# Value and sum products of four heads on four 32-column PE tiles, double attention steps, and a first batch turned by the PE

## The chip, the cores and the metric

The kernel runs on one core of a Trainium2 chip. The metric is device time in microseconds (us) of one execution, as a median of several runs; a profile of one execution goes with every kernel. PE is TensorE (matmul), PEld its weight loads, DVE is VectorE, ACT is ScalarE, POOL is GpSimd, SP is SyncE, which here only issues DMA.

## The reference

Causal attention with 16 extra "beacon" keys that every query sees, then a feed-forward network (FFN) with a gate. Everything comes in float32; the kernel computes in bfloat16 with float32 sums.

```python
B, H, S, Nb, D = 8, 8, 576, 16, 64            # batches, heads, tokens, beacons, head size
scores = (q @ concat(beacon_k, k).T) / sqrt(D) # causal mask on the last S keys
a = exp(scores - max) ; a /= a.sum()
x = (a @ concat(beacon_v, v))                  # -> 4608 tokens x 512 channels
out = (relu(x @ w_gate) * (x @ w_val)) @ w_out # 512 -> 1536 -> 512
```

## The kernel before

Scores are made with keys on the partitions, so that the exponentials `e` can be the moving operand of the value product without a transposition. An attention step handles one pair of heads and one or two key tiles: score matmuls (two row halves of PE, one for each head), one exponential on ACT, masks on POOL; one step later the value and sum products. A batch has 16 steps. One group of FFN work (eight matmuls "up", or twelve "down") is put into each step.

```python
def qk(pr, i):                                   # scores: 64 rows of PE for each head
    s = s_ps.tile([P, 2, 512], FP32, name="s")
    for (kt, q0, n, c, _, _) in STEPS[i]:
        for a in range(2):
            rows = slice(a * D, (a + 1) * D)
            nc.tensor.matmul(s[:, a, c:c + n], pr.batch.kT[rows, pr.p, kt * P:(kt + 1) * P],
                             pr.batch.qT[rows, pr.p, q0:q0 + n], start=True, stop=True)
...
def av(pr, i):                                   # values and sums: two tiles of 64 columns
    ...
        for part in range(2):
            for a in range(2):
                rows = slice(a * D, (a + 1) * D)
                w = pr.batch.v[:kr, kt, c0:c0 + D] if part == 0 else ones[:kr, :]
                nc.tensor.matmul(o[rows, part, q0 - cq0:q0 - cq0 + n], w, e[:kr, a, c:c + n], ...)
    if i == last:
        nc.vector.reciprocal(r[:, :cn], o[:, 1, :cn])
        nc.vector.tensor_mul(xT[:, pr.p, t0:t0 + cn], o[:, 0, :cn], r[:, :cn])
        nc.sync.dma_start(rsum[g:g + 2, cq0:cq0 + cn], ...)      # for a range check at the end
                                                                 # (the general path behind it is not taken here)
...
def up(self, nf, c0, c1):                        # FFN: two accumulators from a ring of two banks
    g = f_ps.tile([P, M_TILE], FP32, name="f")   # four matmuls with wg
    nc.scalar.activation(gs[:, :n], g[:, :n], AF.Relu)
    u = f_ps.tile([P, M_TILE], FP32, name="f")   # four matmuls with wv
    nc.vector.tensor_mul(self.h[:, nf, c0:c1], gs[:, :n], u[:, :n])
...
# K and Q, all batches: load (SP) -> cast to bf16 -> DMA transpose (SP)
nc.sync.dma_start_transpose(dst[:, :, t * P:t * P + n], self.h[x, t][:n])
# step s: scores and exponential of step s, one FFN group, value products of step s - 1
```

Of the kernel before, what the change touches and what calls it, by code (L numbers as in the profile page):

```python
# [15 lines left out]








STEPS = (
    ((0, 0, 240, 0, 112, 16), (1, 112, 128, 240, 128, 0)),
    ((0, 240, 256, 0, 0, 0), (1, 240, 256, 256, 0, 0)),
    ((2, 240, 256, 0, 128, 0), (3, 368, 128, 256, 128, 0)),
    ((0, 496, 80, 0, 0, 0), (1, 496, 80, 80, 0, 0), (2, 496, 80, 160, 0, 0),
     (3, 496, 80, 240, 0, 0), (4, 496, 80, 320, 80, 0)),
)  # L30
STEP_COLS = (368, 512, 384, 400)

CHUNKS = ((0, 240, 0, 0), (240, 256, 1, 2), (496, 80, 3, 3))
CHUNK_OF_STEP = (0, 1, 1, 2)


def general_path(tc, q, k, v, beacon_k, beacon_v, out, ident, wg, wv, wo):
# [76 lines left out]
    x_b = xT_dram.rearrange("(b ko e) d s -> b (e d) ko s", b=B, e=2)  # L114
    out_b = out.rearrange("(b s) n -> b s n", b=B)
    HALF = S // 2
    with tc.tile_pool(name="gen_sb2", bufs=1) as sb, \
# [3 lines left out]
        for ki in range(KM):  # L121
            nc.sync.dma_start(x[:, ki], x_b[bass.ds(i, 1), :, ki].rearrange("o p s -> (o p) s"))
# [12 lines left out]
        for t in range(NT):  # L135
            n = min(P, S - t * P)
            op = ps.tile([P, d_model], FP32, name="g_op")
            for nf in range(NF):
                nc.tensor.matmul(op[:n], hT[:, nf, t * P:t * P + n], wo[:, nf, :],
                                 start=(nf == 0), stop=(nf == NF - 1))  # L140
            ob = sb.tile([P, d_model], FP32, name="g_ob")
            nc.vector.tensor_copy(ob[:n], op[:n])
            nc.sync.dma_start(
                out_b[bass.ds(i, 1), t * P:t * P + n].rearrange("o s n -> (o s) n"), ob[:n])

@with_exitstack
def kernel(
# [23 lines left out]
    TAIL = Stot - 4 * P  # L171
    M_TILE = 512
    scale = 1.0 / (D ** 0.5)
    assert (Nb, S, D) == (16, 576, 64)
# [4 lines left out]
    ones = const.tile([P, D], BF16, name="ones")  # L179
# [5 lines left out]

    rsum = const.tile([2 * B * NP, S], FP32, name="rsum")
# [5 lines left out]
    psb = main.enter_context(tc.tile_pool(name="psb", bufs=3))  # L192
    nrm = main.enter_context(tc.tile_pool(name="nrm", bufs=3))
# [3 lines left out]
    o_ps = main.enter_context(tc.tile_pool(name="o_ps", bufs=2, space=bass.MemoryType.PSUM))  # L197
    f_ps = main.enter_context(tc.tile_pool(name="f_ps", bufs=2, space=bass.MemoryType.PSUM))



    class Batch:
# [28 lines left out]
        def cast(self, x, t, copy):  # L231
            n = self.rows(x, t)
            if x == "v":
                dst = self.v[:n, t]
            else:
                h = self.h[x, t] = half.tile([P, d_model], BF16, name="half")
                dst = h[:n]
            copy(dst, self.raw[x, t][:n])  # L238

        def turn(self, x, t):  # L240
            n = self.rows(x, t)
            dst = self.qT if x == "q" else self.kT
            nc.sync.dma_start_transpose(dst[:, :, t * P:t * P + n], self.h[x, t][:n])  # L243
# [3 lines left out]
    def load_w(dst, src, n0, n1):  # L247
        nc.gpsimd.dma_start(dst[:, :, n0:n1],
                            src.rearrange("(ko ki) n -> ki ko n", ki=P)[:, :, n0:n1])


    class Pair:
        def __init__(self, batch, p):
            self.batch, self.p = batch, p
            self.s, self.e, self.o = {}, {}, {}

    def qk(pr, i):
        s = s_ps.tile([P, 2, 512], FP32, name="s")
        for (kt, q0, n, c, _, _) in STEPS[i]:
            for a in range(2):  # L260
                rows = slice(a * D, (a + 1) * D)
                nc.tensor.matmul(s[:, a, c:c + n],  # L262
                                 pr.batch.kT[rows, pr.p, kt * P:(kt + 1) * P],
                                 pr.batch.qT[rows, pr.p, q0:q0 + n], start=True, stop=True)
        pr.s[i] = s

    def softmax(pr, i):
        n = STEP_COLS[i]
        e = psb.tile([P, 2, 512], BF16, name="e")
        nc.scalar.activation(e[:, :, :n], pr.s[i][:, :, :n], AF.Exp, scale=scale)  # L270
        for (kt, q0, _, c, m, base) in STEPS[i]:
            if m:
                nc.gpsimd.affine_select(  # L273
                    out=e[:, :, c:c + m], in_=e[:, :, c:c + m],
                    pattern=[[0, 2], [1, m]], compare_op=ALU.is_ge, fill=0.0,
                    base=base, channel_multiplier=-1)
        pr.e[i] = e

    def av(pr, i):
        ci = CHUNK_OF_STEP[i]  # L280
        cq0, cn, first, last = CHUNKS[ci]
        if i == first:
            pr.o[ci] = o_ps.tile([P, 2, 256], FP32, name="o")
        o = pr.o[ci]
        e = pr.e[i]
        for j, (kt, q0, n, c, _, _) in enumerate(STEPS[i]):
            kr = min(P, Stot - kt * P)
            for part in range(2):
                for a in range(2):
                    rows = slice(a * D, (a + 1) * D)  # L290
                    c0 = (2 * pr.p + a) * D
                    w = pr.batch.v[:kr, kt, c0:c0 + D] if part == 0 else ones[:kr, :]
                    nc.tensor.matmul(  # L293
                        o[rows, part, q0 - cq0:q0 - cq0 + n], w, e[:kr, a, c:c + n],
                        start=(i == first and j == 0 and part == 0),
                        stop=(i == last and j == len(STEPS[i]) - 1),
                        skip_group_check=True)
        if i == last:
            r = nrm.tile([P, 256], FP32, name="r")
            nc.vector.reciprocal(r[:, :cn], o[:, 1, :cn])  # L300
            t0 = pr.batch.b * S + cq0
            nc.vector.tensor_mul(xT[:, pr.p, t0:t0 + cn], o[:, 0, :cn], r[:, :cn])  # L302
            g = 2 * (pr.batch.b * NP + pr.p)
            nc.sync.dma_start(rsum[g:g + 2, cq0:cq0 + cn],  # L304
                              r.rearrange("(a x) n -> a x n", a=2)[:, 0, :cn])


    class Ffn:
# [21 lines left out]
        def down(self, ms):  # L330
# [7 lines left out]
            nc.sync.dma_start(out[m:m + P, :], ob)  # L338

        def groups(self, c0, c1, d0, d1):  # L340
            return ([lambda nf=nf: self.up(nf, c0, c1) for nf in range(NF)]
                    + [lambda ms=ms: self.down(ms) for ms in range(d0, d1)])

    def count_in_range():

        rows = 2 * B * NP
# [6 lines left out]
        cnt_ps = o_ps.tile([1, 1], FP32, name="o")  # L353
# [6 lines left out]

    ffn_tiles = [Ffn(m * M_TILE) for m in range(n_tokens // M_TILE)]
    W_PARTS = 4
    weights = [lambda d=d, s=s, c=c: load_w(d, s, c * (d_ff // W_PARTS), (c + 1) * (d_ff // W_PARTS))
               for c in range(W_PARTS) for d, s in ((wg, moe_w_gate), (wv, moe_w_val))]
    weights.append(lambda: load_w(wo, moe_w_out, 0, d_model))

    with tc.manual_schedule():
        batches = [Batch(0)]
        copies = {"k": nc.vector.tensor_copy, "q": nc.scalar.copy, "v": nc.gpsimd.tensor_copy}
        for u in UNITS[:6]:  # L370
            batches[0].load(*u)
        for u in UNITS[:6]:
            batches[0].cast(*u, copies[u[0]])
            if u[0] != "v":
                batches[0].turn(*u)
        for w in weights[:2]:
            w()
        for u in UNITS[6:]:
            batches[0].load(*u)


# [5 lines left out]
        for j, u in enumerate(UNITS[6:]):  # L387
            at(j // 3, lambda u=u: batches[0].cast(*u, copies[u[0]]))
            if u[0] != "v":
                at(j // 3, lambda u=u: batches[0].turn(*u))  # L390
        for j, w in enumerate(weights[2:]):
            at(j, w)

        def fetch(b, s0):
            at(s0, lambda: batches.append(Batch(b)))
            for j, u in enumerate(UNITS):
                s = s0 + j * 3 // 4
                at(s, lambda u=u: batches[b].load(*u))
                at(s + 2, lambda u=u: batches[b].cast(*u, nc.gpsimd.tensor_copy))
                if u[0] != "v":  # L400
                    at(s + 3, lambda u=u: batches[b].turn(*u))

        work, ready = [], {}
        for b in range(B):
            for c, (_, _, first, last) in enumerate(CHUNKS):
                for p in range(NP):
                    for i in range(first, last + 1):
                        work.append((b, p, i))
                done = (b * S + CHUNKS[c][0] + CHUNKS[c][1])
                ready[len(work)] = done  # L410
            if b + 1 < B:
                fetch(b + 1, 16 * b + (1 if b else 3))


        spans = [(0, 240), (240, 512)] + [(m, m + M_TILE) for m in range(M_TILE, n_tokens, M_TILE)]
        queue, have, pairs = [], 0, {}
        LAG = 1
        for s in range(len(work) + LAG):
            if s - LAG in ready:
                have = ready[s - LAG]  # L420
# [5 lines left out]
            for act in later.pop(s, []):  # L426
                act()
            if s < len(work):
                b, p, i = work[s]
                pr = pairs.setdefault((b, p), Pair(batches[b], p))  # L430
                qk(pr, i)
                softmax(pr, i)
            if queue:
                queue.pop(0)()
# [42 lines left out]
```

## Time and profile before

| kernel before | |
|---|---|
| time | 477.17 us, median of 3 (474.74 to 478.57) |
| profiled span | 476.9 us |
| PE busy | 407.7 us, 85% |
| DVE, ACT, POOL busy | 235.9, 197.5, 132.9 us |

Three parts of the profile page of the kernel before: busy time by engine, and the span in 40 slices of 11.9 us (a digit is the busy share in tenths; PEclk is the clock granted to PE).

```profile
PE 407.7 (85%) x3454; PEld 198.3 (42%) x3505; DVE 235.9 (49%) x322; ACT 197.5 (41%) x290; POOL 132.9 (28%) x293
...
PE   0043748979999999999999999999999999799994
...
PEclk9999759979999999999999999999999999899998
...
GB/s 164 188 200 195 162 184 117 133 194 102 111 119 194 96 104 151 160 83 112 155 161 91 112 139 167 79 123 175 127 95 3 1 24 68 0 1 88 1 18 76
```

There are two regimes. For about 80 us PE is idle for long stretches, and DMA moves 160 to 200 GB/s for most of that time. From there to the end PE is full. So a change must either shorten the start or take PE time away.

The waits of PE in the first 100 us of the kernel before (who waited for what: us in all, times, longest) show what the start waits for, and the windows show each 20 us of it (columns: busy us of PE, PEld, DVE, ACT, POOL with counts, granted clock, DMA share, GB/s).

```profile
PE o L293 <- POOL e L273: 26.8, 8, 8.4
PE s L262 <- DMA qT<-half: 18.3, 2, 17.2
```

```profile
20.00:40.00 20.00, 6.09 (x53) 3.63 (x53) 9.62 (x11) 6.40 (x9) 9.71 (x18) 1.00 1.34 198
40.00:60.00 20.00, 13.07 (x105) 7.72 (x104) 6.66 (x10) 6.48 (x11) 4.82 (x9) 0.83 1.24 180
60.00:80.00 20.00, 11.64 (x170) 8.08 (x171) 7.91 (x13) 5.58 (x10) 8.37 (x17) 0.74 1.05 167
```

The first score product waits 17.2 us for a turned Q; after that the value products wait for masks.

One step in the steady stretch, from the timeline of PE of the kernel before (start, us until the modelled end, line, matmul, how many):

```profile
229.94 0.30 PE L293 MATMUL o<-e,v 128*64 128x256 bf16 x2
230.07 0.28 PE L293 MATMUL o<-e,ones 128*64 128x256 bf16 x2
230.18 0.28 PE L293 MATMUL o<-e,v 128*64 128x256 bf16 x2
230.29 0.28 PE L293 MATMUL o<-e,ones 128*64 128x256 bf16 x2
230.50 0.39 PE L262 MATMUL s<-qT,kT 64*128 64x256 bf16 x4
230.83 1.04 PE L320 MATMUL f<-xT,wg 128*128 128x512 bf16 x4
231.70 1.03 PE L326 MATMUL f<-xT,wv 128*128 128x512 bf16 x4
232.66 0.30 PE L293 MATMUL o<-e,v 128*64 128x256 bf16 x2
```

Read it by the starts, since the ends overlap. A pair of 256-column value matmuls takes 0.11 us and then the next pair starts; four 512-column FFN matmuls take 0.87 us. From the start of the last quartet (231.70) to the next value matmul (232.66) it is 0.96 us instead of 0.87: about 0.1 us is lost where the shape of the tiles changes, and again from values to scores and from scores to FFN.

The two groups of the kernel before that the change aims at, beside the FFN (line, engine, operation, count, busy us, mean ns of one, idle time before and its releaser):

```profile
L300 DVE RECIPROCAL r<-o 128x240 f32<-128x240 f32 (+2 forms) x96 | 130.0, 1354 | 89.0 <-PE o L293 86.5
...
L293 PE MATMUL o<-e,v 128*64 128x80 bf16 (+3 forms) x704 | 66.6, 246 | 33.4 <-POOL e L273 33.4
```

### The profile page before, as it was taken

The page shows a single profiled execution, that of the slowest core. Times are in us where ns is not written, and L with a number is a line of the kernel's source. Part 1 is how long each engine was busy: PE and PEld are TensorE (multiplying, and loading weights), DVE is VectorE, ACT ScalarE, POOL GpSimd, SP SyncE. Part 2 cuts the span into 40 slices and gives each one's busy share as a digit, 9 for nine tenths or more (in the row PEclk, how much of TensorE's full clock was granted, in tenths as well). Part 3 has the DMA queues.
Part 4 walks back from the last instruction along what each step waited for, and adds up shares of the span by engine and source line. Part 5 has one row for each costly group of instructions (what it writes and reads, how often), then busy time and mean ns, then how long its engine had stood idle before and what let it go on. Part 6 is the DMA issues. An engine that isn't in the chain of part 4 may idle for free.

```text
span 476.9 us, 9059 instructions
## 1 busy us (share of the span) xinstructions
PE 407.7 (85%) x3454; PEld 198.3 (42%) x3505; DVE 235.9 (49%) x322; ACT 197.5 (41%) x290; POOL 132.9 (28%) x293
## 2 busy tenths in 40 slices
PE   0043748979999999999999999999999999799994
PEld 0022425545444444444444444444444444244442
DVE  0052426745486357546663766286528653330320
ACT  2132414534455455445544555455545543132321
POOL 2171235444234333423351334143411110000000
PEclk9999759979999999999999999999999999899998
DMA  9999998695359337934892498258720001002002
GB/s 164 188 200 195 162 184 117 133 194 102 111 119 194 96 104 151 160 83 112 155 161 91 112 139 167 79 123 175 127 95 3 1 24 68 0 1 88 1 18 76
DMA packets 166145, 53.37 MB, mean 112 GB/s; under 512 B 155728, under 2 KB 161488, under 8 KB 166096
## 3 DMA queue, kind: packets, MB, share of 16 engines
q1 hardware_dynamic: 160320, 48.01, 50.2%
q0 software_dynamic: 5776, 4.72, 7.0%
q8 instruction: 29, 0.48, 0.4%
q14 instruction: 20, 0.16, 0.1%
HBM read 38.27 MB, written 9.44 MB: 100 GB/s over the span
## 4 chain that ended last, share of the span: by engine, by line
PE 57%; DMA 20%; SPq 9%; DVE 5%; POOL 4%; issue 3%; ACT 0%; POOLq 0%; DVEq 0%; ACTq 0%
PE f L333 20%; PE f L320 13%; PE f L326 12%; DMA raw<-in_k_dram 12%; PE o L293 8%; DMA raw<-in_q_dram 6%; SPq L220 5%; PE s L262 4%; DVE r L300 3%; SPq L243 3%; DMA raw<-in_v_dram 2%; POOL half L238 2%; POOL e L273 2%; SPq L304 1%; DVE xT L302 1%
## 5 line engine op out<-in xcount | busy, mean ns | idle before, releaser
L300 DVE RECIPROCAL r<-o 128x240 f32<-128x240 f32 (+2 forms) x96 | 130.0, 1354 | 89.0 <-PE o L293 86.5
L270 ACT ACTIVATE e<-s 128x736 bf16<-128x736 f32 (+3 forms) x128 | 110.5, 864 | 135.9 <-PE s L262 125.7
L328 DVE TENSOR_TENSOR hT<-g,f 128x512 bf16<-128x512 f32 (+2 forms) x120 | 75.6, 630 | 110.0 <-PE f L326 98.1
L320 PE MATMUL f<-xT,wg 128*128 128x512 bf16 (+2 forms) x453 | 116.3, 369 | 5.3 <-DVE xT L302 3.1
L326 PE MATMUL f<-xT,wv 128*128 128x512 bf16 (+2 forms) x473 | 115.4, 365 | 1.6 <-ACT g L323 0.7
L333 PE MATMUL f<-wo,hT 128*128 128x512 bf16 x415 | 96.5, 380 | 1.5 <-issue 1.0
L293 PE MATMUL o<-e,v 128*64 128x80 bf16 (+3 forms) x704 | 66.6, 246 | 33.4 <-POOL e L273 33.4
L273 POOL TENSOR_SCALAR_AFFINE_SELECT e<-e 128x256 bf16<-128x256 bf16 (+2 forms) x160 | 58.9, 387 | 106.4 <-ACT e L270 106.2
L323 ACT ACTIVATE g<-f 128x512 f32<-128x512 f32 (+2 forms) x120 | 66.3, 553 | 43.4 <-PE f L320 39.5
L293 PEld LDWEIGHTS <-v 128*64 128x64 bf16 (+1 forms) x704 | 38.0, 112 | 84.0 <-issue 82.6
L326 PEld LDWEIGHTS <-wv 128*128 128x128 bf16 x480 | 48.1, 100 | 57.0 <-issue 12.1
L238 POOL CAST half<-raw 128x512 bf16<-128x512 f32 (+1 forms) x70 | 42.7, 611 | 88.2 <-DMA raw<-in_q_dram 39.3
L262 PE MATMUL s<-qT,kT 64*128 64x80 bf16 (+2 forms) x704 | 47.4, 239 | 18.3 <-DMA qT<-half 18.3
L293 PE MATMUL o<-e,ones 128*64 128x80 bf16 (+3 forms) x704 | 61.3, 238 | 0.0
L320 PEld LDWEIGHTS <-wg 128*128 128x128 bf16 x480 | 40.1, 100 | 47.3 <-issue 17.8
L333 PEld LDWEIGHTS <-hT 128*128 128x128 bf16 x432 | 40.0, 98 | 46.8 <-issue 0.8
L336 ACT COPY ob<-f 128x512 f32<-128x512 f32 x36 | 21.1, 586 | 70.0 <-PE f L333 67.0
L238 POOL CAST v<-raw 128x512 bf16<-128x512 f32 (+1 forms) x40 | 24.5, 611 | 66.9 <-DMA raw<-in_v_dram 66.8
L293 PEld LDWEIGHTS <-ones 128*64 128x64 bf16 (+1 forms) x704 | 36.5, 114 | 0.2
L302 DVE TENSOR_TENSOR xT<-o,r 128x240 bf16<-128x240 f32 (+2 forms) x96 | 34.3, 358 | 3.3
L262 PEld LDWEIGHTS <-kT 64*128 64x128 bf16 x704 | 18.5, 97 | 33.5 <-issue 25.2
L238 DVE CAST half<-raw 128x512 bf16<-128x512 f32 (+1 forms) x5 | 2.3, 460 | 21.6 <-DMA raw<-in_k_dram 21.6
(19 smaller groups left out, 17.0 us busy)
## 6 DMA issues: line engine op xcount, KB each, us to landing
out_dram<-ob SPq DMA_DIRECT2D x36, 256.0 KB
raw<-in_q_dram SPq DMA_DIRECT2D x32, 256.0 KB
raw<-in_k_dram SPq DMA_DIRECT2D x24, 256.0 KB
raw<-in_v_dram SPq DMA_DIRECT2D x24, 256.0 KB
raw<-in_k_dram SPq DMA_DIRECT2D x8, 224.0 KB
raw<-in_v_dram SPq DMA_DIRECT2D x8, 224.0 KB
wg<-in_moe_w_gate_dram POOLq DMA_DIRECT2D x4, 384.0 KB, 6.1
wv<-in_moe_w_val_dram POOLq DMA_DIRECT2D x4, 384.0 KB, 7.6
```

The lines of the kernel that those rows point to most:

```text
L238: copy(dst, self.raw[x, t][:n])
L262: nc.tensor.matmul(s[:, a, c:c + n], pr.batch.kT[rows, pr.p, kt * P:(kt + 1) * P], pr.batch.qT[rows, pr.p, q0:q0 + n], start=True, stop=True)
L270: nc.scalar.activation(e[:, :, :n], pr.s[i][:, :, :n], AF.Exp, scale=scale)
L273: nc.gpsimd.affine_select(out=e[:, :, c:c + m], in_=e[:, :, c:c + m], pattern=[[0, 2], [1, m]], compare_op=ALU.is_ge, fill=0.0, base=base, ...
L293: nc.tensor.matmul(o[rows, part, q0 - cq0:q0 - cq0 + n], w, e[:kr, a, c:c + n], start=(i == first and j == 0 and part == 0), stop=(i == la ...
L300: nc.vector.reciprocal(r[:, :cn], o[:, 1, :cn])
L302: nc.vector.tensor_mul(xT[:, pr.p, t0:t0 + cn], o[:, 0, :cn], r[:, :cn])
L320: nc.tensor.matmul(g[:, :n], wg[:, ki, nf * P:(nf + 1) * P], x[:, ki], start=(ki == 0), stop=(ki == KM - 1))
L323: nc.scalar.activation(gs[:, :n], g[:, :n], AF.Relu)
L326: nc.tensor.matmul(u[:, :n], wv[:, ki, nf * P:(nf + 1) * P], x[:, ki], start=(ki == 0), stop=(ki == KM - 1))
L328: nc.vector.tensor_mul(self.h[:, nf, c0:c1], gs[:, :n], u[:, :n])
L333: nc.tensor.matmul(o, self.h[:, nf, ms * P:(ms + 1) * P], wo[:, nf, :], start=(nf == 0), stop=(nf == NF - 1))
```

## The change

The intent has four parts. (1) Values and sums of four heads run on four tiles of 32 columns: three parts (lower half of the values, upper half, sums) instead of two parts for each of two pairs, so three column times where there were four. (2) Steps are twice as large: 7 a batch instead of 16, with about 4.5 us of FFN work in each; value products are made for a whole chunk (240, 256 or 80 queries of four heads) at once, when all its key tiles are done. (3) K and Q of the first batch are loaded in halves and turned by PE (matmul with an identity) instead of DMA transposes. (4) One reciprocal serves four heads: 48 instead of 96, of the same length. A consequence: the channels lie in another order on the partitions, so the gate and value weights come in four loads of 32 partitions each where one load was enough. Smaller changes of the order of work came with it (more buffers for the exponentials, other steps for loads and casts, later stores).

```diff
-        for part in range(2):
-            for a in range(2):
-                rows = slice(a * D, (a + 1) * D)
-                w = pr.batch.v[:kr, kt, c0:c0 + D] if part == 0 else ones[:kr, :]
-                nc.tensor.matmul(o[rows, part, ...], w, e[:kr, a, c:c + n], ...)
+                for part in range(3):
+                    for hh in range(4):
+                        rows = slice(hh * C, (hh + 1) * C)            # C = 32
+                        c0 = (2 * hh + self.g) * D + part * C
+                        w = ones[:kr, :] if part == 2 else self.batch.v[:kr, kt, c0:c0 + C]
+                        o = self.os[rows] if part == 2 else self.ab[rows, part]
+                        nc.tensor.matmul(o[:, ...], w, e[:kr, 2 * (hh % 2) + hh // 2], ...)
 ...
     def load_w(dst, src, n0, n1):
-        nc.gpsimd.dma_start(dst[:, :, n0:n1], src.rearrange("(ko ki) n -> ki ko n", ki=P)[:, :, n0:n1])
+        for hh in (0, 2, 1, 3):
+            nc.gpsimd.dma_start(dst[hh * C:(hh + 1) * C, :, n0:n1],
+                src[hh * P:(hh + 1) * P, n0:n1].rearrange("(k p) n -> p k n", p=C))
 ...
+        def turn_half(self, x, i, cast, move):           # first batch only
+            ... cast to bf16 ...
+            for r in range(2):
+                for j in range(NP):
+                    nc.tensor.transpose(ps[:, j, r], h[:, r, j * P:(j + 1) * P], ident)
+            move(dst[...], ps.rearrange("a j r p -> a j p r"))
 ...
+    STEPS = 7
+    QUOTA = 4.5
+        # step: scores of two units, first exponential; values of the finished chunks, reciprocal;
+        #       FFN groups for about 4.5 us, after the first of them scaling and second exponential
+                if u[0] != "v":
+                    at(s + (1 if b == 1 else 2), lambda u=u: batches[b].turn(*u))
```

## The prediction

> **What bounds it now.** PE is busy 407.7 of 476.9 us (busy table). By windows, the first 100 us hold only about 50 us of PE work, part of it at a granted clock of 0.74 to 0.83; from 100 to 400 us PE is busy 94 to 99%. In the chain of waits the start is DMA (raw K, Q loads, DMA transposes); the first score matmul starts at 17.2 us, waiting for the transposed Q; value products wait 33.4 us for the mask on POOL, 14 times, up to 8.4 us. After that PE is the limit.
>
> In the steady stretch (timeline, 204 to 250 us) a step takes about 2.6 us: eight FFN matmuls at 0.217 us (1.74), values and sums 0.32 to 0.43, scores 0.16 to 0.21, and 0.33 left at the three changes of tile shape (about 0.1 us between the last FFN matmul's end and the first value matmul, and so on). The Trainium skill ("TensorEngine Tiling (Array Packing)", Key Properties) says a change of tiling mode drains the engine; these gaps agree. With 128 steps that is about 42 us. DVE reciprocals take 130 us; PE hardly waits for them.
>
> **What changes, costed.**
> 1. 56 steps for 128: 72 x 0.33 = 24 us of shape changes saved. Several FFN groups now stand back to back; in the FFN-only end a group takes 1.87 us, not 1.74, because the second accumulator waits for the DVE product: 5 to 7 us given back.
> 2. Values and sums: now 1664 columns x 2 parts on two tiles, about 1.43 us a pair, 46 us in all. On four tiles 1664 x 3 parts for 16 groups would stream in 33 us. But loads and matmuls rise from 2816 to 4224; an 80-column pair takes 36 ns for four instructions, so eight in 33 ns may not fit. I estimate 38 to 44 us: gain about 5, all on PE. The skill ("TensorE: Matmul & The Clock Gate", Part 3) measured 2.38 times for three column tiles, also below ideal.
> 3. Reciprocals: 48 instead of 96 of the same length, DVE -65 us, off the critical path, worth almost nothing.
> 4. Start: K and Q of batch 0 by PE; first score matmul at 11 to 12 us. But FFN cannot start before step 3, and needs weights: 34 issues instead of 9, in POOL's queue; from the second group on, each waits for an earlier one's landing (6 to 8 us measured), with masks and casts behind it. So POOL will stall value products until 50 to 60 us. DMA, about 180 GB/s, is full there in both kernels. I expect 8 to 18 us gained over the first 100 us.
> 5. Later waits for POOL shrink by some microseconds.
>
> **Sum.** 477 - 24 + 6 - 5 - 13 - 6 = 435; I say 434 us, range 412 to 454 (8 in 10). Chances: faster 0.94, within 2% 0.04, slower 0.02.
>
> **What would show it.** (1) In the steady stretch a step of about 6 us, a batch of 42 us instead of 46, the same 0.3 us of gaps per step. (2) Four 256-column value matmuls in about 0.11 us, four 80-column ones in 0.05 to 0.07. (3) DVE busy near 165 us. (4) First score matmul near 11 us; waits for POOL masks and weights before 60 us.
>
> **What would make it wrong.** Four-column tiles that don't overlap (values over 60 us: then only 3 to 5% faster); POOL blocked by weights for longer, so batch 1 starts late; a throttled clock in the denser stretch. Conversely, if POOL keeps up and weights land early, 410 us.

## The result, and the profile after

The changed kernel took 442.77 us (median of 4, 441.67 to 442.96) against 477.87 us (median of 4, 474.74 to 478.62) for the kernel before on the same chip. The ratio is 0.926, with an interval from 0.923 to 0.930.

The same parts of the page, now of the changed kernel; a slice is 11.0 us:

```profile
PE 384.0 (87%) x4202; PEld 198.1 (45%) x4253; DVE 174.9 (40%) x232; ACT 190.7 (43%) x272; POOL 132.5 (30%) x242
...
PE   3487552898799999999999999999999999699994
...
PEclk9999765699699999999999999999999999999999
...
GB/s 240 222 115 189 132 152 165 164 180 149 82 156 168 100 137 189 141 101 175 166 105 117 156 167 128 120 147 187 120 64 3 2 73 26 0 25 71 1 26 77
```

PE now starts at once, but a hole opens in the fifth to seventh slice (44 to 77 us), where the granted clock also falls. DMA moved 240 GB/s in the first slice and only 115 in the third.

Waits of PE in the first 100 us of the changed kernel, the four longest, and the windows that answer to those of before:

```profile
PE f L412 <- DMA wo<-in_moe_w_out_dram: 8.1, 2, 5.8
PE f L291 <- DVE half L288: 7.6, 3, 3.6
PE s L322 <- DMA qT<-half: 5.7, 1, 5.7
PE ab L364 <- POOL e L338: 3.7, 1, 3.7
```

```profile
20.00:40.00 20.00, 15.37 (x165) 10.74 (x166) 10.23 (x16) 8.68 (x14) 18.83 (x35) 1.00 1.05 142
40.00:60.00 20.00, 10.13 (x109) 6.23 (x110) 4.71 (x8) 3.05 (x6) 4.61 (x7) 0.75 0.99 166
60.00:80.00 20.00, 8.32 (x194) 5.38 (x193) 1.96 (x4) 5.10 (x6) 7.94 (x15) 0.59 0.62 131
```

The mask waits are nearly gone. In their place PE waits for weights, for one turned tile of the second batch, and for rows of the first (of the 7.6 us, 3.1 are the first wait of all, for the beacon keys, and 4.5 are for the last rows). From 20 to 40 us POOL is busy 18.8 of 20 us.

One step of the changed kernel in its steady stretch, PE's timeline (each `ab` line holds the two value parts of four heads, each `os` line their sums):

```profile
218.79 0.52 PE L322 MATMUL s<-qT,kT 64*128 64x80 bf16 x12
219.25 0.40 PE L364 MATMUL ab<-e,v 128*32 128x256 bf16 x8
219.47 0.28 PE L364 MATMUL os<-e,ones 128*32 128x256 bf16 x4
219.58 0.39 PE L364 MATMUL ab<-e,v 128*32 128x256 bf16 x8
...
222.25 1.03 PE L399 MATMUL f<-xT,wg 128*128 128x512 bf16 x4
223.26 1.02 PE L405 MATMUL f<-xT,wv 128*128 128x512 bf16 x4
224.22 0.61 PE L322 MATMUL s<-qT,kT 64*128 64x128 bf16 x12
224.76 0.26 PE L364 MATMUL ab<-e,v 128*32 128x80 bf16 x8
224.84 0.21 PE L364 MATMUL os<-e,ones 128*32 128x80 bf16 x4
```

Two value parts of four heads, 256 columns each, take 0.22 us (219.25 to 219.47) and the sums 0.11 us. So four matmuls take 0.11 us, as two did before. Even with 80 columns two parts take 0.08 and the sums about 0.04 us: eight instructions (four loads, four matmuls) in 0.04 us. In the second FFN group of the step the `wv` quartet starts 1.01 us after the `wg` quartet, not 0.87 (222.25 to 223.26).

The groups that answer to those of before:

```profile
L372 DVE RECIPROCAL r<-os 128x240 f32<-128x240 f32 (+2 forms) x48 | 65.2, 1358 | 108.9 <-PE os L364 84.0
...
L364 PE MATMUL ab<-e,v 128*32 128x80 bf16 (+4 forms) x1408 | 44.9, 244 | 6.3 <-POOL e L338 3.7
```

Where along the run was it gained? The last scaling of a batch on DVE marks the end of its attention. Those of the first and the last batch, from the DVE timeline of the kernel before, then of the changed one:

```profile
82.75 0.24 DVE L302 TENSOR_TENSOR xT<-o,r 128x80 bf16<-128x80 f32 x1
...
400.76 0.24 DVE L302 TENSOR_TENSOR xT<-o,r 128x80 bf16<-128x80 f32 x1
```

```profile
76.07 0.32 DVE L377 TENSOR_TENSOR xT<-ab,r 128x160 bf16<-128x160 f32 x1
...
372.15 0.32 DVE L377 TENSOR_TENSOR xT<-ab,r 128x160 bf16<-128x160 f32 x1
```

The second batch ends at 126.9 us before and at 120.4 after (same view). So of the 35.7 us between the two spans, 6.6 were won by the end of the first batch, none in the second, 22.0 in the next six (3.7 a batch), and 7.2 in the FFN that is left at the end: 21 "up" groups instead of 24 (counted by their products on DVE), and three groups at the 1.87 us that a group takes there are 5.6 us.

For the steady stretch of five batches I added up, from the traces, the time from each PE matmul's start to the next one's, by kind (126.9 to 356.2 us before, 120.3 to 331.5 us after):

| us in five batches | before | after |
|---|---|---|
| values and sums | 26.8 | 20.8 |
| scores | 10.3 | 12.1 |
| FFN | 137.6 (60 up, 20 down) | 155.3 (63 up, 20 down) |
| intervals in which the tile shape changes | 54.4 (240 of them) | 22.8 (100 of them) |
| sum | 229.1 | 210.9 |

An interval with a change holds the streaming of the matmul before it as well (0.217 us for FFN; before, on average 0.062 for the last pair of scores and of values in a step; after, 0.078 for the last pair of scores and 0.047 for the last four of values; all from their columns at 512 in 0.216 us). Without that, the changes take 54.4 - 80 x 0.341 = 27.1 us before and 22.8 - 35 x 0.295 - 30 x 0.047 = 11.1 us after: 0.11 us each in both. Values and sums, with their last matmuls, are 31.8 and 22.2 us; some waits for masks are in the 31.8.

### The profile page after: what moved, and what is told of

It reads as the page before. It is cut to its first block, busy times and chain, and to the rows that moved or that the text cites. A ratio compares the mean times of both kernels' runs of the same rounds, so it can differ in the third digit from the quotient of the medians.

```text
span 441.2 us, 10205 instructions
## 1 busy us (share of the span) xinstructions
PE 384.0 (87%) x4202; PEld 198.1 (45%) x4253; DVE 174.9 (40%) x232; ACT 190.7 (43%) x272; POOL 132.5 (30%) x242
## 3 DMA queue, kind: packets, MB, share of 16 engines
q0 software_dynamic: 6176, 4.72, 7.4%
## 4 chain that ended last, share of the span: by engine, by line
PE 79%; DMA 8%; DVE 5%; issue 3%; POOL 2%; SPq 1%; ACT 1%; DVEq 0%; POOLq 0%; ACTq 0%
PE f L405 23%; PE f L412 21%; PE f L399 20%; PE ab L364 6%; DMA raw<-in_q_dram 6%; PE s L322 5%; PE os L364 3%; DMA raw<-in_v_dram 2%; DVE r L372 2%; DVE hT L407 1%; SPq L232 1%; POOL v L247 1%; DVE xT L377 1%; DVE half L288 1%; POOL e L338 1%
## 5 line engine op out<-in xcount | busy, mean ns | idle before, releaser
L330 ACT ACTIVATE e<-s 128x1024 bf16<-128x1024 f32 (+2 forms) x112 | 105.4, 963 | 42.1 <-PE s L322 42.1
L372 DVE RECIPROCAL r<-os 128x240 f32<-128x240 f32 (+2 forms) x48 | 65.2, 1358 | 108.9 <-PE os L364 84.0
L338 POOL TENSOR_SCALAR_AFFINE_SELECT e<-e 128x512 bf16<-128x512 bf16 (+2 forms) x80 | 46.8, 596 | 186.1 <-ACT e L330 175.9
L364 PE MATMUL ab<-e,v 128*32 128x80 bf16 (+4 forms) x1408 | 44.9, 244 | 6.3 <-POOL e L338 3.7
L322 PE MATMUL s<-qT,kT 64*128 64x80 bf16 (+3 forms) x704 | 36.8, 243 | 9.1 <-DMA qT<-half 5.7
L364 PE MATMUL os<-e,ones 128*32 128x80 bf16 (+4 forms) x704 | 36.6, 243 | 0.0
L364 PEld LDWEIGHTS <-v 128*32 128x32 bf16 (+1 forms) x1408 | 28.4, 102 | 16.3 <-issue 8.2
L377 DVE TENSOR_TENSOR xT<-ab,r 128x480 bf16<-128x480 f32 (+2 forms) x48 | 26.5, 553 | 0.7
L364 PEld LDWEIGHTS <-ones 128*32 128x32 bf16 (+1 forms) x704 | 20.3, 105 | 0.4
L298 POOL DMA_DIRECT2D wg<-in_moe_w_gate_dram x16 | 8.9, 586 | 0.0
```

The lines of the kernel that those rows point to most:

```text
L322: nc.tensor.matmul(self.s[:, a, c + j * n:c + (j + 1) * n], self.batch.kT[rows, 2 * g + j, kt * P:(kt + 1) * P], self.batch.qT[rows, 2 * g ...
L330: nc.scalar.activation(e[:, :k * 4 * n].rearrange("p (k a x) -> p a k x", k=k, a=2), self.s[:, :, :k * 2 * n].rearrange("p a (k x) -> p a ...
L338: nc.gpsimd.affine_select(out=cols[:, :, :m], in_=cols[:, :, :m], pattern=[[0, 4], [1, m]], compare_op=ALU.is_ge, fill=0.0, base=base, cha ...
L364: nc.tensor.matmul(o[:, q0 - cq0:q0 - cq0 + n], w, e[:kr, 2 * (hh % 2) + hh // 2], start=(i == 0 and part != 1), stop=(i == self.last), sk ...
L372: nc.vector.reciprocal(self.r[:, :n], self.os[:, :n])
L377: nc.vector.tensor_mul(xT[:, 2 * self.g:2 * self.g + 2, t0:t0 + n], self.ab[:, :, :n], self.r[:, :n].unsqueeze(1).to_broadcast([P, 2, n]))
```

## The experiments

All are edits of the changed kernel and were timed against the kernel before on the same chip. Differences below are between medians and the changed kernel's 442.8 us; the interval of each ratio to the kernel before is given where it decides. Spread between runs of one kernel was 1 to 4 us. The groups ran on different chips, and the kernel before was 1.4 us faster beside e5 to e8 than beside the changed kernel: taken from the ratios, the gains of e5, e6, e7 and e8 are 6.3, 1.3, 6.2 and 4.8 us, about 1 us less than the differences below. No reading depends on that.

### e1: two tiles at a time

```diff
-                for part in range(3):
-                    for hh in range(4):
+                for pair in range(2):
+                    for part, hh in [(x, 2 * pair + y) for x in range(3) for y in range(2)]:
```

> Edit: the same matmuls of the value and sum products, reordered so that only two of the four 32-column tiles are used in turn (head pair 0 with its three parts, then head pair 1), so at most two products can overlap. Theory A: in the changed kernel all four tiles really stream at once (a 256-column part of four matmuls takes 0.11 us in its trace), value and sum products take about 4.4 us a batch, 35 us in all, all on the path of PE; with two at a time they take twice that: about 36 us more, 476 to 480 us. Theory B: what the prediction assumed, that issue of eight instructions is the limit, so that four tiles are worth little over two: 0 to 8 us more, 443 to 451 us.

Measured: 443.1 us, ratio 0.926 (0.922 to 0.930): no difference. It looks like theory B, but the trace shows that the edit failed to do what it was meant to do. PE's timeline of e1, the first products of a chunk:

```profile
219.71 0.41 PE L364 MATMUL ab<-e,v 128*32 128x256 bf16 x8
219.94 0.30 PE L364 MATMUL os<-e,ones 128*32 128x256 bf16 x4
220.05 0.41 PE L364 MATMUL ab<-e,v 128*32 128x256 bf16 x8
```

The program's order is four value matmuls of the first two heads, then their two sums, then four values and two sums of the others. The trace has eight value matmuls first and then four sums. Single starts are 219.708 and 219.711, 219.728 and 219.731, then 219.828, 219.832, 219.848 and 219.851; the first two sums, fifth and sixth in the program, start at 219.937 and 219.940. The trace does not name tiles, but the order fits only if PE started the second pair's matmuls on its idle tiles while the first pair's next ones waited for busy tiles. Nor does the order look fixed in the program: 14 of e1's 16 chunks of 80 columns end in a mixed order of values and sums, the two at 66 and 73 us do not, with the same code. So all four tiles ran at once again, at the same 0.109 us for four. The experiment does not tell the theories apart; e9 was made for that.

### e2: two more changes of tile shape in each step

```diff
-            for u in units:
+            for u in units[:1]:
                 u.qk()
 ...                                   # in the middle of the step's first FFN group:
+            while middle:
+                middle.pop()()        # scores and exponential of the second unit
```

> Edit: the second unit's score products of each step are moved into the middle of the step's first FFN group, which adds two changes of tile shape to each of some 55 steps and no work. Theory A: a change of tile shape costs PE about 0.1 us each (0.096 to 0.15 us net in the traces), so 55 x 2 x 0.11 = 12 us more: 453 to 457 us, and nearly all between 76 and 372 us. Theory B: the changes of shape cost nothing by themselves, and fewer steps helped through fewer waits on other engines: within 3 us of 443.

Measured: 452.8 us, ratio 0.947 (0.943 to 0.950): 10 us more, just under the range of theory A and far from B. The five batches took 218.4 us instead of 210.9, so 7.4 us before rounding for 70 added changes: 0.106 us each, the size that the traces gave. The changes of shape cost PE time by themselves.

### e3: the reciprocals twice

```diff
                         c.scale()
+                        c.again()     # reciprocal of r into an unused tile
```

> Edit: DVE computes a second, unused reciprocal of the same size for each chunk, after the chunk's scaling, so DVE gets back the 65 us of reciprocals that the change removed. Theory A (prediction, step 3): reciprocals are off the critical path, 0 to 4 us more (443 to 447 us), a few tenths for each step in which the extra reciprocal delays the product of the second FFN group. Theory B: halving the reciprocals is a main source of the gain: 12 us more or over.

Measured: 450.3 us, ratio 0.942 (0.938 to 0.946): 7 us more, outside both ranges, so a miss. In the table's terms only FFN grew: 161.1 instead of 155.3 us in five batches. In DVE's timeline the extra reciprocal (1.65 to 1.74 us for the two longer shapes) stands before the product of the next FFN group. PE's waits from 100 to 400 us now list 5.5 us, in eight waits, of `wv` matmuls for ACT's activation, which the changed kernel does not have; how the late product reaches ACT was not followed further. So 65 us more on DVE can cost 7 us when placed there. It does not show that halving them gained anything: in the kernel before PE waited for DVE nowhere in the steady stretch (from 100 to 400 us its waits list only masks, 6.6 us, and issue, 1.0 us).

### e4: the first batch turned by DMA again

```diff
-        first.load_half("k", 0) ... first.turn_half("k", 0, dve, dve) ...
+        for u in UNITS[:6]:
+            first.load(*u)
+        for u in UNITS[:6]:
+            first.cast(*u, copies[u[0]])
+            if u[0] != "v":
+                first.turn(*u)         # DMA transpose
+        ...                            # the other tiles at steps 0 and 1
```

> Edit: K and Q of the first batch are loaded, cast and turned by DMA transposes as in the kernel before; all else as in the changed kernel. First score product at about 17 us instead of 9.6. Theory A: the head start of PE turning is kept to the end: 6 to 9 us more, 449 to 452 us. Theory B: the first 80 us are set by the DMA queues and by POOL, which issues 34 weight loads, and the early scores only wait later for weights and for the second batch: under 3 us more, 443 to 446 us.

Measured: 455.6 us, ratio 0.954 (0.950 to 0.958): 12.8 us more, more than theory A allowed. The first scores start at 13.2 us, not 17. PE's waits in the first 100 us then have at their head:

```profile
PE s L322 <- DMA qT<-half: 34.4, 3, 14.5
```

The batches end about 8 to 10 us later from the first to the last (86.2 instead of 76.1 us, 380.2 instead of 372.2). The profiled execution was the fastest of the four (452.65 us), so its trace shows 10 of the 13 us. Loading in halves and turning by PE, which the edit takes away together, are worth 10 to 13 us, and without them the start of the changed kernel would have been slower than that of the kernel before (first batch done at 86 us against 83).

### e5: the second batch turned one step later

```diff
-                    at(s + (1 if b == 1 else 2), lambda u=u: batches[b].turn(*u))
+                    at(s + 2, lambda u=u: batches[b].turn(*u))
```

> Edit: the DMA transposes of the second batch are issued one step later (as for all later batches), so that SP's queue does not stand behind them (14 us at one of them, 20 to 33 us into the run) while the next loads wait. Theory A: SP standing behind a transpose that waits for a cast on POOL starves DMA between 20 and 30 us (123 GB/s there) and that sets the end of the first batch: 4 to 10 us less, 433 to 439 us. Theory B: DMA's bandwidth over the whole first 80 us is the limit, or POOL itself: within 2 us of 443.

Measured: 435.5 us, ratio 0.913 (0.909 to 0.918): 7.3 us less, as theory A said. SP's longest wait in the first 100 us, first of the changed kernel, then of e5, and the 20 to 40 us window of e5:

```profile
SPq L255 <- POOL v L247: 16.3, 2, 14.0
```

```profile
SPq L255 <- POOL v L247: 7.8, 2, 6.9
```

```profile
20.00:40.00 20.00, 15.07 (x164) 10.61 (x165) 10.23 (x17) 8.59 (x14) 19.81 (x37) 1.00 1.26 179
```

In the changed kernel SP issued nothing between 20.5 and 33.5 us. POOL issued eight weight loads from 28.5 to 32.8 us and only then cast the tile; the transpose, which had waited 14 us for it, went out at 33.5, and the loads of further tiles, which stood behind it, from 36.2. In e5 the first of these loads goes out at 21.9 us. With the transpose later, DMA moves 179 instead of 142 GB/s in that window, and the first batch ends at 70.4 us instead of 76.1.

### e6: casts of the second batch on DVE and ACT

```diff
-                at(s + 1, lambda u=u: batches[b].cast(*u, pool))
+                at(s + 1, lambda u=u: batches[b].cast(*u, {"k": dve, "q": act, "v": pool}[u[0]] if b == 1 else pool))
```

> Edit: the casts of the second batch's K go to DVE and of its Q to ACT instead of POOL, which is busy 88 to 100% from 10 to 40 us with casts, masks and the issue of weight loads. Theory A: POOL's in-order queue is what holds up the second batch: its first transpose is issued at about 22 us instead of 33.5, DMA is fuller from 20 to 40 us, 4 to 10 us less, 433 to 439 us. Theory B: DMA bandwidth is the limit: within 2 us of 443. A miss the other way is possible too: a cast that waits for DMA on DVE or ACT holds up FFN.

Measured: 440.3 us, ratio 0.924 (0.919 to 0.928), against 0.926 (0.923 to 0.930) of the changed kernel: 2.5 us less, within noise, between both theories. POOL's queue was part of the hold-up: the first transpose came at 27.6 us instead of 33.5, though not at 22. But the miss that was foreseen happened too. PE's waits in the first 100 us begin with

```profile
PE f L399 <- ACT g L402: 12.9, 2, 12.7
```

FFN's activations stood behind a cast on ACT. The wait moved from one in-order queue to another.

### e7: half of the weight bytes

```diff
-                dst[hh * C:(hh + 1) * C, :, n0:n1], src[hh * P:(hh + 1) * P, n0:n1]...
+                dst[hh * C:(hh + 1) * C, :, n0:(n0 + n1) // 2], src[hh * P:(hh + 1) * P, n0:(n0 + n1) // 2]...
```

> Edit: each weight load moves half of its columns, the other half is set to zero by DVE at the start; as many issues as before, half of the bytes. The result is wrong on purpose. Theory A: the first 80 us are limited by the bytes that DMA must move: about 4.7 MB less to read at about 180 GB/s is up to 20 us of DMA time, so 8 to 20 us less, 423 to 435 us. Theory B: order and waits in the queues of POOL and SP are the limit: 0 to 4 us less, 439 to 443 us.

Measured: 435.1 us, ratio 0.913 (0.910 to 0.917), result wrong as intended: 7.7 us less, between the two ranges. From 20 to 40 us DMA moved 83 GB/s, so its rate was not the limit there; weights that land sooner do help. The clearing on DVE at the start also delayed its casts (PE's wait for them grew from 7.6 to 10.7 us), so the gain is if anything understated. How much of it bytes are stays open. Theory A counts the weights as float32 (4.7 MB less), but the profile's GB/s count them as bfloat16: the weights' queue moved 2.36 MB instead of 4.72. At 180 GB/s that is 13 us, and 7.7 us are more than half of it.

### e8: the FFN-only end

```diff
-            u = f_ps.tile([P, M_TILE], FP32, name="f")
+            u = acc()                  # in the FFN-only end: a score bank, idle by then
 ...
             if j == 4:
-                in_range = count_in_range()
+                ok = count_in_range()  # DVE part
+            if j == 8:
+                in_range = count(ok)   # matmul and read
```

> Edit: in the end that holds FFN alone the second accumulator of each group uses the idle score banks, and the matmul of the range check comes four groups later than its DVE work. Theory A: in that end a group takes 1.87 us instead of 1.74 because the second accumulator waits for DVE's product in the same bank (24 groups: 3 us), and the range check costs PE another 2.8 us: together 5 to 6 us less, 436 to 438 us. Theory B: the 1.87 us is the matmuls' own pace (weights or clock): only the 2.8 us, 440 us.

Measured: 437.4 us, ratio 0.916 (0.911 to 0.922): 5.4 us less, as theory A said. PE's timeline of e8 in the end:

```profile
400.86 1.03 PE L410 MATMUL s<-xT,wv 128*128 128x512 bf16 x4
401.72 1.03 PE L404 MATMUL f<-xT,wg 128*128 128x512 bf16 x4
```

Quartets now start 0.86 us apart. The 1.87 us of a group in the end was the wait for the bank, not the pace of the matmuls.

### e9: a fourth slot

```diff
-                for part in range(3):
+                for part in range(4):
 ...
+                        w = zeros[:kr, :] if part == 3 else ...      # added onto the sums
```

> Edit: a fourth part for each key tile, four matmuls with zero weights added onto the sums, so that value and sum products take as many column times as on two tiles (4 x 1664 columns for each of 16 groups, as 2 parts x 2 pairs before). The result stays right. Theory A: the four tiles stream at one column per clock, PE is the limit, so the slot that the change saved is worth 1664 x 16 / 2.4 = 11 us: 452 to 455 us. Theory B (the prediction's number): the issue of instructions takes the place of the saved slot, so that the change gained only 5 us there; then sixteen instructions in a slot group run at the issue limit too and the extra part costs more than its columns on 80-column groups (over 0.05 us each): over 456 us. Theory C: PE has slack in the attention steps: under 447 us.

Measured: 456.4 us, ratio 0.955 (0.952 to 0.958): 13.6 us more, at the edge between the ranges of A and B, so the trace has to decide. Five batches took 218.2 us instead of 210.9 between the same marks, 7.3 us or 1.45 us a batch; the 2 x 1664 columns of the extra part at 2.37 columns per ns (512 in 0.216 us, FFN) are 1.40 us. For eight batches that is 11.6 us. The profiled spans differ by 14.0 us: 3.7 by the end of the second batch, 8.7 in the next six, and 1.6 in the FFN at the end, which took 70.3 us here, 68.7 in the changed kernel's trace and 68.6 to 71.1 in those of e1 to e7 and e12, so that part may be noise. PE's timeline of e9 in an 80-column chunk:

```profile
232.06 0.21 PE L366 MATMUL os<-e,ones 128*32 128x80 bf16 x4
232.09 0.21 PE L366 MATMUL os<-e,zeros 128*32 128x80 bf16 x4
232.13 0.25 PE L366 MATMUL ab<-e,v 128*32 128x80 bf16 x8
```

An 80-column slot of four loads and four matmuls starts every 0.03 to 0.04 us, with no slot of the kind over 0.05 us that B asked for. The saved slot was worth its columns, about 11 us, and no issue limit ate it.

### e10 and e11: what can be kept

e10 is e5 and e8 together; e11 turns the last 64 rows of the first batch at step 3 as well:

```diff
-        at(1, lambda: first.turn_rows(tail_k, ...))
+        at(3, lambda: first.turn_rows(tail_k, ...))
```

> Edit: e5 (second batch turned one step later) and e8 (FFN-only end on the score banks, range check later) together. If the two gains are at different places and independent (-7.3 and -5.4 us), 429 to 431 us; if the earlier start only meets another limit, 434 us or more.

> Edit: e10, and the last 64 rows of K and Q of the first batch are turned by PE at step 3 instead of step 1, because PE waits 7.6 us in its queue for their cast (which waits for the load) while they are needed only at step 5. Theory A: the waiting time is lost, scores of step 2 start at about 18.5 us instead of 23.3, and 2 to 5 us are kept: 425 to 428 us. Theory B: weights' landing sets when FFN can go, so nothing is kept: 429 to 431 us.

Measured: e10 428.8 us, ratio 0.898 (0.895 to 0.901): the two gains add up. e11 427.5 us, ratio 0.894 (0.891 to 0.897): 1.2 us less than e10 with overlapping intervals, so unclear, and below what theory A wanted. The expectation had the wait wrong: of the 7.6 us, 3.1 are for the beacon keys at the start, which the edit leaves as they are, and only 4.5 for these rows. The edit also moves their cast to step 3 together with the turning, so PE still waits 3.1 us for it there, and only 1.5 us of waiting are gone. Both versions are right in their results, and they are the fastest here: 10 to 11% under the kernel before.

### e12: fewer weight loads

```diff
-        w_actions = [... load_w(d, s, n, n + 384) for n in range(0, d_ff, 384) ...]
+        w_actions = [... load_w(d, s, n, n + 768) for n in range(0, d_ff, 768) ...]
 ...
-            at(1 + j // 2, w)
+            at((1, 1, 4, 4)[j], w)
```

> Edit: the gate and value weights come in 16 loads of 768 columns instead of 32 of 384, the second half at step 1, the down weights at step 4 as before; same bytes. POOL spends 0.55 us on each issue, 18 us in all in the first 40 us. Theory A (the prediction's mechanism, step 4): POOL's issues, and its waits for earlier landings, hold up casts and masks: 3 to 8 us less, 435 to 440 us. Theory B: what holds up the first 80 us is SP standing behind transposes and the landings themselves, and the first FFN group now has to wait for twice the bytes: within 2 us of 443, or slower.

Measured: 436.0 us, ratio 0.912 (0.910 to 0.915): 6.8 us less, as theory A said. The issue of one load keeps POOL 0.56 us for twice the bytes (0.59 us before), so the issues fell from 17.7 to 8.9 us of POOL time. The 20 to 40 us window of e12:

```profile
20.00:40.00 20.00, 14.98 (x164) 10.23 (x165) 9.78 (x15) 8.39 (x14) 11.09 (x21) 1.00 1.24 196
```

POOL is busy 11.1 us there instead of 18.8, DMA moves 196 GB/s, and the first batch ends at 69.1 us. SP's longest wait is still 11.9 us. The edit also asks for the second half of these weights earlier (at step 1, not at steps 1 to 3), so fewer issues and earlier weights are not told apart. Whether e12 and e5 win the same 7 us or different ones was not run and stays open.

## Why the prediction was right or wrong

The time, 442.8 us against 434 predicted, lies in the range, and the direction was right. Split by where it was gained, the prediction had 13 us for the start and 29 us for everything later (24 - 6 + 5 + 6); measured were 6.6 us by the end of the first batch (6.5 by the end of the second) and 29.2 us later. So step 4 was sized too large, and step 2 too small. That the later sum came out right is luck: two errors cancelled. The five batches of the table save 18.2 us and hold three "up" groups more (5.2 us), so 4.7 us a batch, where 29 / 8 = 3.6 was predicted (the tiles, point 2); but the first two batches, held up by their data, show none of it (in e5, with its data earlier, the second batch takes 41.1 us instead of 44.0). The two experiments that measured the parts alone account for most of it: 28 changes of shape fewer a batch at 0.106 us (e2) and 1.45 us for the slot (e9), together 4.4 us.

1. **Shape changes: right.** Predicted 24 us. The table gives 27.1 - 11.1 = 16.0 us in five batches, about 25 us if scaled to eight, and e2 shows that a change costs 0.106 us by itself. The drain on a change of tiling mode, which the Trainium skill states ("TensorEngine Tiling (Array Packing)", Key Properties), agrees; the page has no figure. The give-back was 5 to 7 us in the prediction; in the table an "up" group takes 1.716 us before ((137.6 + 80 x 0.217 - 20 x 2.6) / 60) and 1.760 us after, computed the same way with 35 and 63: 2.7 us in five batches, 4 to 5 in eight. e8 showed the named cause, the wait for the bank, in the FFN-only end.
2. **Values and sums: too small.** Predicted a gain of 5 us, because eight instructions in 33 ns "may not fit". They fit: an 80-column slot took about 0.036 us, and e9 put the worth of the saved slot at 11.6 us. The failed step is the issue limit that was read from four instructions in 36 ns: that pair was limited by its columns (80 / 2.37 = 34 ns), so its time said nothing about issue.
3. **Reciprocals: right as far as shown.** DVE lost 65 us of them. No wait of PE in the steady stretch of the kernel before was for DVE. The direct test (e3) put the time back at another place and measured the place.
4. **Start: mechanism half right, size too large.** First scores at 9.6 us were even earlier than the 11 to 12 predicted, and e4 puts loading in halves and PE turning at 10 to 13 us. The weight loads in POOL's queue do cost time, as feared: half as many issues gained 7 us (e12). But they did not act as the prediction said. The waits for earlier landings did not come: POOL was idle 0.0 us before the 32 gate and value loads, and their issue alone took 17.7 us. Nor did value products wait for masks until 50 to 60 us: those waits fell from 26.8 to 3.7 us. The loads acted through SP: casts late on POOL, transposes waiting for the casts, loads waiting behind the transposes (14 us at one of them), so DMA ran at 142 GB/s from 20 to 40 us, while the prediction called it full there in both kernels. e5 loosened that link (longest wait 6.9 us instead of 14.0) and gained 7.3 us. After that PE waited for weights and the second batch at a clock of 0.59 to 0.75. The clock is an observation; what it cost alone was not measured.
5. **Later mask waits: right.** 6.6 us from 100 to 400 us before, none in that stretch after.

## What to carry to other kernels

Read the worth of a tiling change from column times and from the gaps at shape changes, both measured by the starts of matmuls; a time that is equal to its columns says nothing about an issue limit. When a change shortens the start of one engine, follow the in-order queues that feed it: here a DMA transpose in SP's queue, waiting for a cast on a POOL that was busy issuing weight loads, held back loads that had nothing to do with it, and one step more of delay for the transpose gained 7 us. An experiment by order of instructions needs its trace read before its time is believed, because the engine may run another order.

## What the Trainium skill lacked or had wrong

- "TensorE: Matmul & The Clock Gate", Part 3, says that matmuls start strictly in program order. In e1 the first two sums, fifth and sixth in the program, started at 219.937 and 219.940 us, after eight value matmuls (219.708 to 219.851), of which four stand behind those sums in the program: matmuls for other column tiles overtook them. In the changed kernel the trace keeps the order of the program. A single semaphore on the last matmul of such a group rests on that rule; the runs do not show whether ends keep the order, since ends are modelled.
- The same part says that a weight load overlaps matmuls in flight only when the row group differs (and, some lines before, that the background weight buffer allows it too). Here all loads of value and sum products use all 128 rows, and twelve loads and twelve matmuls of 256 columns take 0.33 us (219.25 to 219.58), 0.109 us for each four, which is the column time alone.
- The same part measured 2.38 times for three column tiles, by the span of one pack. Four tiles here, in a sustained stream and by starts, reached 4 x 256 columns in 0.109 us, 9.4 columns per ns against 2.37 of a full-array FFN matmul: 3.96 times.
- "TensorEngine Tiling (Array Packing)" states the drain on a mode change but no cost: 0.106 us for each change in e2, 0.11 us in both traces.
